# Numerators of an attention stage: two matmuls of 64 channels by 128 tokens per unit in place of four of 64 by 64

## The chip, the cores and the metric

The kernel runs on one core of one Trainium2 chip. The metric is the device time of one execution in microseconds (us). A core has a TensorE (in the profile PE for its matmuls, PEld for its weight loads), a VectorE (DVE), a ScalarE (ACT), a GpSimd (POOL) and a queue engine (SP) that here only issues transfers. A matmul multiplies a stationary operand ("weights", loaded by a LDWEIGHTS instruction of its own) by a moving operand that is streamed past it, and writes to PSUM, which has eight banks.

## What is computed

Linear attention over 8 batches of 8 heads, 576 tokens and 64 channels, and then a feed-forward layer with a tanh GELU over all 4608 tokens:

```python
q_p, k_p = (phi(q), phi(k))                      # phi(x) = x + 1 if x > 0 else exp(x)
kv  = np.einsum('bhsd,bhse->bhde', k_p, v)
z   = np.sum(k_p, axis=2)
num = np.einsum('bhsd,bhde->bhse', q_p, kv)
den = np.einsum('bhsd,bhd->bhs', q_p, z)[..., None] + 1e-06
attn_out = num / den
...
h = x @ w_in                                     # 4608x512 by 512x2048
g = gelu_tanh(h)
out = g @ w_out                                  # 2048x512
```

The kernel adds a column of ones to v, so that one product gives the numerator (64 columns) and the denominator (column 65) of a head. This product, of phi(q) with the 64 by 65 matrix `kv` of its head, is called n below; the sum over tokens that makes that matrix is called kv.

## The kernel before

Each batch gives its first 512 tokens to an iteration of its own (j = 0 to 7); the remaining 64 tokens of the eight batches make a ninth one (j = 8). An iteration is 16 groups of h (four 128x128 by 128x512 matmuls each, line 384) and 16 groups of o (four such matmuls each, line 725): for j from 2 on, all of h and then o by blocks of 128 tokens. The attention of a later batch is put between these groups by hand: `at(j, slot, fn)` keeps a function for a slot, and `run` calls it when the loop of `iteration` gets there. Nothing is scheduled by a planner: every engine runs its instructions in the order in which the program issues them, and semaphores hold it only for data and for free buffers.

`plan_attention(b)` puts the attention of batch b, for b = 3 to 7, at slot 17 of iteration b - 1, which is behind the second group of o. For b = 8 it puts the attention of the ninth iteration (the remaining tokens) at slot 17 of iteration 7. Each time it calls `nab_quads(qt_cs, bs, kv_b)`, which issues, one behind the other on TensorE,

- n: 16 units (c, i, a), one for each block c of 128 tokens and each pair of heads 2a + i, with four matmuls each: t for two halves of 64 tokens, s for the two heads of the pair. The weights are 64 channels by 64 tokens of the transposed phi(q) (`qt`, line 324), the moving operand is the 64 by 65 matrix of the head (`kv_of_head`, line 325), and the output goes to 64 partitions of a bank, s = 0 and s = 1 to different banks. Six units fill a pair of banks, and the last four go to a pair of their own (`n_pair`).
- kv of the batch after, where there is one (b = 3 to 6): 72 matmuls with weights of 64 tokens by 64 channels and a moving operand of 64 by 65 (`kv_paired`, line 249), four at a time on the four quarters of the array.

The function that `nab_quads` returns, `x_of`, then divides the numerators by their denominators on VectorE (lines 282 and 283), issues the four transposing transfers of the result on SP (line 665) and copies kv out of PSUM (line 347).

The halves t exist because in the ninth iteration a block of 128 tokens holds 64 tokens of one batch and 64 of the next, and so `bs[c]` names two batches and the two halves need different matrices. For b = 3 to 7 `bs[c]` is (b, b).

Of the kernel before, what the change touches and what calls it, by code (L numbers as in the profile page):

```python
# [15 lines left out]
def kernel(  # L16
# [20 lines left out]
    P = 128  # L37
    HP = P // 2
# [40 lines left out]
    def bank(name, shape, dt=FP32):  # L79
        return ps_b.tile(shape, dt, name=name, tag="b")  # L80

    def pair_of_banks(name):
        return ps_a.tile([P, 2, 512], FP32, name=name, tag="a")
# [159 lines left out]
    def kv_paired(b, ii, kv_of):  # L243
        kp, vp = phi["k", b], vp_paired(b)
        for j in range(J):
            for s in range(2):
                for a in range(2):
                    r, u = slice(HP * a, HP * (a + 1)), 2 * ii + s
                    nc.tensor.matmul(  # L249
                        kv_of(a, ii)[HP * s : HP * (s + 1)],  # L250
                        lhsT=kp[r, j, u, :],
                        rhs=vp[r, j, u, :],
                        start=(j == 0),
                        stop=(j == J - 1),
                        skip_group_check=True,
                    )
# [15 lines left out]
    def kv_of_head(b, s, i):  # L272

        r = slice(HP * s, HP * (s + 1))
        return kvs[b][r, i, :] if b > 2 else kvbds[b][r, i, E * s : E * (s + 1)]

    def divide(x_v, n_v):

        heads = tuple(slice(None) for _ in n_v.shape[:-1])
        shape = list(n_v.shape[:-1])  # L280
        r = psm.tile(shape, FP32, name="r" + "".join(str(d) for d in shape[1:]))
        nc.vector.reciprocal(r, n_v[heads + (D,)])  # L282
        nc.vector.tensor_tensor(  # L283
            x_v,
            n_v[heads + (slice(0, D),)],
            r[heads + (None,)].to_broadcast(shape + [D]),
            op=ALU.mult,
        )
# [20 lines left out]
    def nab_quads(qt_cs, bs, kv_b):  # L309

        ns = [[bank("n_ps", [P, 6 * E]) for _ in range(2)] for _ in range(2)]
        n_pair = pair_of_banks("n_ps")
        ns.append([n_pair[:, s] for s in range(2)])
        units = [(c, i, a) for c in range(C) for i in range(2) for a in range(2)]
        for n, (c, i, a) in enumerate(units):
            g = n // 6
            for t in range(2):
                for s in range(2):  # L320
                    cs = slice(HP * t, HP * (t + 1))
                    nc.tensor.matmul(  # L322
                        ns[g][s][cs, E * (n - 6 * g) : E * (n - 6 * g + 1)],
                        lhsT=qt_cs[c][HP * s : HP * (s + 1), 2 * a + i, cs],
                        rhs=kv_of_head(bs[c][t], s, 2 * a + i),
                        skip_group_check=True,
                    )
        if kv_b is not None:
            for ii in range(2):
                kv_paired(kv_b, ii, lambda a, ii: n_pair[:, a, E * (4 + ii) : E * (5 + ii)])  # L330

        def x_of(transposed):
            x = pxs.tile([P, C, d_model], BF16, name="xs")
            x_v = x.rearrange("p c (i s a d) -> p s (c i) a d", s=2, a=2, d=D)
            for g in range(2):
                for s in range(2):
                    divide(
                        x_v[:, s, 3 * g : 3 * (g + 1)],
                        ns[g][s].rearrange("p (k a e) -> p k a e", a=2, e=E),
                    )  # L340
                for c in ((0,), (1, 2))[g]:
                    transposed(c, x[:, c])
            n_v = n_pair[:, :, 0 : 4 * E].rearrange("p s (k a e) -> p s k a e", a=2, e=E)
            divide(x_v[:, :, 6:8], n_v)
            transposed(3, x[:, 3])
            if kv_b is not None:
                nc.vector.tensor_copy(
                    out=kvs[kv_b].rearrange("p (a i) e -> p a i e", a=2),
                    in_=n_pair[:, :, 4 * E : 6 * E].rearrange("p a (i e) -> p a i e", e=E),
                )  # L350

        return x_of
# [314 lines left out]
    def plan_attention(b):  # L667


        def attention():  # L670
            if b < B:
                bs = [(b, b)] * C
                x_of = nab_quads([qts[b][:, c] for c in range(C)], bs, b + 1 if b + 1 < B else None)
                x_of(lambda c, x: transposed_x(b, c, x))
            else:
                x_of = nab_quads(rest_qt, [(2 * m, 2 * m + 1) for m in range(C)], None)
                x_of(
                    lambda m, x: nc.sync.dma_start_transpose(
                        out=xt_rest[:, :, P * m : P * (m + 1)], in_=x
                    )  # L680
                )

        at(b - 1, 17, attention)
# [145 lines left out]
```

## Time and profile before

| | before |
|---|---|
| median of 4 runs | 283.92 us (283.90 to 284.55) |
| the profiled execution: its own time | 284.09 us |
| the profiled execution: its span | 282.3 us |
| mean granted TensorE clock | 0.998 |
| TensorE matmuls at line 322 (n) | 384, in six stretches |
| of these, batches 3 to 7 | 320, in five stretches |
| TensorE weight loads at line 322 | 384 |
| TensorE matmuls at line 249 (kv), behind an n | 288, in four stretches |

The span goes from the first to the last instruction of the program; the time of an execution has 1.8 us more around it. In the views, a line of a timeline gives the start and the length of a group of like instructions in us, the engine, the source line, the operation, output<-inputs, the shapes and the count; in brackets stands idle time before it. The length of a group runs to the end of its last instruction, and a matmul's end is modelled: successive matmuls overlap. "64*64" and "128*128" are the part of the array that an instruction uses, rows by columns. Some records of matmuls can be missing from a trace.

### The profile page before, as it was taken

The numbers are of one execution on the slowest core, as the hardware profiler recorded it, in microseconds if no ns is written. First come the engines' busy times: TensorE is split into PE (matmuls) and PEld (weight loads), VectorE is DVE, ScalarE is ACT, GpSimd is POOL, SyncE is SP. The second block draws the span as 40 slices with busy tenths as digits, with TensorE's granted clock in tenths as the row PEclk, the third lists the DMA queues.
The fourth block names the chain that finished last, engine by engine and source line by source line (L and its number), as shares of the span: only waits on it lengthen the run. The fifth ranks groups of instructions, "written<-read, shape, count | busy, mean of one in ns | idle before, by whom it ended". The sixth has DMA issues, their size and how long they took to land.

```text
span 282.3 us, 5435 instructions
## 1 busy us (share of the span) xinstructions
PE 273.6 (97%) x2311; PEld 135.4 (48%) x2341; DVE 102.6 (36%) x177; ACT 164.1 (58%) x224; POOL 15.0 (5%) x21
## 2 busy tenths in 40 slices
PE   8799999999999999999999999999999999999995
PEld 3474455445444544454445444544444444444444
DVE  3850386334955850356034640350114001400001
ACT  4678878785986915692569346832682364026400
POOL 3147200000000000000000000000000000000000
PEclk9999999999999999999999999999999999999999
DMA  7999999967999987907695640066405300420022
GB/s 244 401 406 396 411 401 404 404 250 219 176 386 266 297 152 216 377 22 170 179 386 122 155 129 0 2 118 179 115 2 148 114 0 2 138 85 0 2 74 74
DMA packets 59591, 53.83 MB, mean 191 GB/s; under 512 B 35760, under 2 KB 45360, under 8 KB 59568
## 3 DMA queue, kind: packets, MB, share of 16 engines
q1 hardware_dynamic: 56784, 44.58, 52.1%
q10 hardware_dynamic: 2784, 8.91, 8.8%
q8 instruction: 18, 0.29, 0.4%
q14 instruction: 5, 0.04, 0.0%
HBM read 36.70 MB, written 9.44 MB: 163 GB/s over the span
## 4 chain that ended last, share of the span: by engine, by line
PE 93%; DMA 3%; issue 1%; SPq 1%; DVE 1%; ACT 0%
PE h_ps L384 44%; PE o_ps L725 44%; DMA v_x<-in_v_dram 3%; PE n_ps L322 1%; PE kv_ps L249 1%; PE n_ps L249 1%; PE n_ps L265 1%; PE t_ps L377 1%; SPq L95 1%; SPq L100 0%; PE t_ps L530 0%; DVE vp L238 0%; DVE x L367 0%; DVE kvbd L261 0%; DVE o_sb L686 0%
## 5 line engine op out<-in xcount | busy, mean ns | idle before, releaser
L725 PE MATMUL o_ps<-w_out_sb,g 128*128 128x512 bf16 (+2 forms) x588 | 126.0, 367 | 1.6 <-issue 0.9
L384 PE MATMUL h_ps<-xt,w_in_sb 128*128 128x512 bf16 (+1 forms) x556 | 113.2, 359 | 0.5 <-issue 0.2
L394 ACT ACTIVATE g<-h_ps 128x512 bf16<-128x512 f32 x144 | 84.4, 600 | 36.5 <-PE h_ps L384 35.0
L384 PEld LDWEIGHTS <-w_in_sb 128*128 128x128 bf16 x628 | 58.5, 98 | 64.7
L725 PEld LDWEIGHTS <-g 128*128 128x128 bf16 x608 | 57.4, 98 | 63.4
L686 ACT COPY o_sb<-o_ps 128x512 f32<-128x512 f32 (+1 forms) x19 | 10.8, 575 | 65.7 <-PE o_ps L725 52.6
L686 DVE COPY o_sb<-o_ps 128x512 f32<-128x512 f32 (+1 forms) x19 | 12.2, 645 | 50.5 <-PE o_ps L725 45.6
L282 DVE RECIPROCAL r<-n_ps 128x6 f32<-128x6 f32 (+2 forms) x43 | 8.2, 191 | 59.8 <-PE n_ps L322 54.3
L227 DVE TENSOR_SCALAR k_p<-k_x 128x2304 bf16<-128x2304 f32 (+1 forms) x9 | 11.0, 1221 | 24.9 <-DMA k_x<-in_k_dram 24.9
L283 DVE TENSOR_TENSOR xs<-n_ps,r 128x384 bf16<-128x384 f32 (+1 forms) x30 | 17.5, 584 | 1.0
L219 ACT ACTIVATE k_e<-k_x 128x2304 bf16<-128x2304 f32 (+1 forms) x9 | 17.1, 1902 | 1.0 <-DMA k_x<-in_k_dram 0.9
L219 ACT ACTIVATE q_e<-q_x 128x2048 bf16<-128x2048 f32 (+1 forms) x9 | 15.5, 1719 | 3.0 <-DMA q_x<-in_q_dram 2.9
L227 DVE TENSOR_SCALAR q_p<-q_x 128x2048 bf16<-128x2048 f32 (+1 forms) x9 | 9.9, 1102 | 13.4 <-DMA q_x<-in_q_dram 13.4
L384 PE MATMUL h_ps<-xt_rest,w_in_sb 128*128 128x512 bf16 x63 | 13.9, 379 | 0.1
L233 DVE TENSOR_TENSOR q_p<-q_p,q_e 128x2048 bf16<-128x2048 bf16 (+1 forms) x9 | 9.9, 1100 | 6.9 <-ACT q_e L219 6.8
L407 ACT ACT_TABLE_LOAD x9 | 11.5, 1283 | 0.2
L233 DVE TENSOR_TENSOR k_p<-k_p,k_e 128x2304 bf16<-128x2304 bf16 (+1 forms) x9 | 11.0, 1220 | 1.2 <-ACT k_e L219 0.8
L238 DVE CAST vp<-v_x 128x2304 bf16<-128x2304 f32 (+1 forms) x9 | 11.0, 1223 | 0.6 <-DMA v_x<-in_v_dram 0.6
L219 ACT ACT_TABLE_LOAD x8 | 10.3, 1283 | 0.1
L416 PE MATMUL w_ps<-warm 128*128 128x512 bf16 x31 | 9.0, 450 | 1.2 <-DVE warm L181 1.2
L139 POOL CAST w_in_sb<-w_st 128x512 bf16<-128x512 f32 (+2 forms) x6 | 7.6, 1269 | 14.7 <-DMA w_st<-in_moe_w_in_dram 14.7
L283 DVE TENSOR_TENSOR x<-n_ps,r 128x512 bf16<-128x512 f32 (+1 forms) x13 | 7.9, 609 | 0.4
(50 smaller groups left out, 77.5 us busy)
## 6 DMA issues: line engine op xcount, KB each, us to landing
out_dram<-o_sb ACTq DMA_DIRECT2D x16, 512.0 KB, 3.2
k_x<-in_k_dram SPq DMA_DIRECT2D x7, 1152.0 KB, 7.2
v_x<-in_v_dram SPq DMA_DIRECT2D x7, 1152.0 KB, 11.8
q_x<-in_q_dram SPq DMA_DIRECT2D x6, 1024.0 KB, 9.5
w_st<-in_moe_w_in_dram SPq DMA_DIRECT2D x3, 1024.0 KB, 13.3
q_x<-in_q_dram SPq DMA_DIRECT2D x4, 512.0 KB, 8.8
w_st<-in_moe_w_out_dram SPq DMA_DIRECT2D x2, 1024.0 KB, 12.7
w_st<-in_moe_w_out_dram SPq DMA_DIRECT2D x4, 512.0 KB, 11.2
```

What stands on the lines that cost most here:

```text
L219: nc.scalar.activation(o, i, AF.Exp)
L227: nc.vector.tensor_scalar(o, i, 1.0, 1.0, op0=ALU.add, op1=ALU.max)
L233: nc.vector.tensor_tensor(p, p, e, op=ALU.min)
L238: fn(out=vp_paired(b)[:, :, us, 0:D].rearrange("p j u d -> p u j d"), in_=ld["v", b][:, us].rearrange("p u (j d) -> p u j d", d=D),)
L282: nc.vector.reciprocal(r, n_v[heads + (D,)])
L283: nc.vector.tensor_tensor(x_v, n_v[heads + (slice(0, D),)], r[heads + (None,)].to_broadcast(shape + [D]), op=ALU.mult,)
L384: nc.tensor.matmul(h_ps[:, ts], lhsT=w_in_sb[:, c, P * m : P * (m + 1)], rhs=xt[:, c, ts], start=(c == 0), stop=(c == KM - 1), skip_group_ ...
L394: nc.scalar.activation(g[:, m, :], h_ps, AF.Gelu_apprx_tanh)
L407: nc.scalar.preload_act_table_set("gelu_apprx_tanh_and_others")
L416: nc.tensor.matmul(w_ps, lhsT=warm[:, 0:P], rhs=warm)
L686: (nc.scalar.copy if on_scalar else nc.vector.tensor_copy)(dst, src)
L725: nc.tensor.matmul(o_ps, lhsT=g[:, m, P * t : P * (t + 1)], rhs=w_out_sb[:, m, fs], start=(m == 0), stop=(m == MM - 1),)
```

## The change

Where both halves of a block belong to the same batch (batches 3 to 7), the loop over t is run once, with all 128 tokens as weights: a unit is two matmuls (s = 0, 1) of 64 channels by 128 tokens with an output of 128 partitions, in place of four of 64 by 64 with an output of 64 partitions. The ninth iteration's n stays as it was, and so does kv.

```diff
         for n, (c, i, a) in enumerate(units):
             g = n // 6
-            for t in range(2):
+            one = bs[c][0] == bs[c][1]
+            for t in range(1 if one else 2):
                 for s in range(2):
-                    cs = slice(HP * t, HP * (t + 1))
+                    cs = slice(0, P) if one else slice(HP * t, HP * (t + 1))
                     nc.tensor.matmul(
                         ns[g][s][cs, E * (n - 6 * g) : E * (n - 6 * g + 1)],
                         lhsT=qt_cs[c][HP * s : HP * (s + 1), 2 * a + i, cs],
                         rhs=kv_of_head(bs[c][t], s, 2 * a + i),
```

`HP` is 64, `P` 128 and `E` 65. The five stretches have 160 matmuls and 160 weight loads fewer in all.

## The prediction

> **What bounds the kernel now.** I read the page first, its busy times and its chain of waits, which is followed back from the last instruction:
>
> ```profile
> PE 273.6 (97%) x2311; PEld 135.4 (48%) x2341; DVE 102.6 (36%) x177; ACT 164.1 (58%) x224; POOL 15.0 (5%) x21
> PE 93%; DMA 3%; issue 1%; SPq 1%; DVE 1%; ACT 0%
> ```
>
> TensorE is busy for 97% of the span and is 93% of the chain. A busy PE alone would not prove that it is the bound, so I looked at the same chain in order of time, around one place of the change:
>
> ```profile
> 93.29 0.15 issue
> 93.44 0.76 PE n_ps L322 x64
> 94.20 0.68 PE n_ps L249 x72
> 94.88 0.16 issue
> 95.04 10.74 PE o_ps L725 x49
> ```
>
> From here to the end the chain never leaves TensorE: n, kv, o, h follow each other with no wait for another engine. A nanosecond saved or lost in n is one of the whole time, unless it makes somebody late (see below). Third came the timeline of TensorE around all five places. Three of them, and a kv alone (behind an o and ahead of an o, with no n) for comparison:
>
> ```profile
> 39.87 0.78 PE L249 MATMUL kv_ps<-vp,k_p 64*64 64x65 bf16 x72
> 40.58 0.39 PE L725 MATMUL o_ps<-w_out_sb,g 128*128 128x512 bf16 x1
> ```
> ```profile
> 121.80 0.81 PE L725 MATMUL o_ps<-w_out_sb,g 128*128 128x512 bf16 x3
> 122.54 0.76 PE L322 MATMUL n_ps<-kv,qt 64*64 64x65 bf16 x64
> 123.12 0.86 PE L249 MATMUL n_ps<-vp,k_p 64*64 64x65 bf16 x72
> ```
> ```profile
> 180.75 0.76 PE L322 MATMUL n_ps<-kv,qt 64*64 64x65 bf16 x64
> 181.33 0.84 PE L249 MATMUL n_ps<-vp,k_p 64*64 64x65 bf16 x72
> ```
> ```profile
> 209.83 0.76 PE L322 MATMUL n_ps<-kv,qt 64*64 64x65 bf16 x64
> 210.75 1.46 PE L725 MATMUL o_ps<-w_out_sb,g 128*128 128x512 bf16 x6 [0.16 <-issue]
> ```
>
> The reader is to see three things. First, the same 72 kv matmuls take 0.78 us alone and 0.86 (batch 6: 0.84) behind n. Second, n to its last start: each of these lengths has a tail of 0.19 (a 64x65 matmul's own duration), so n takes 0.57 from first to last start, and kv follows at 122.54 + 0.58. Third, the price of a change between the array as a whole and its four quarters. The last of three 512-wide matmuls starts at 121.80 + 0.81 - 0.38 = 122.23 and n at 122.54, 0.31 later, where 512-wide matmuls follow each other in (0.81 - 0.38)/2 = 0.215: 0.09 lost. Back again, at the kv alone, the last kv starts at 39.87 + 0.78 - 0.19 = 40.46 and o at 40.58: 0.12, of which some 0.03 is that last matmul's own streaming, so 0.09 again. The 0.16 of "issue" behind the other stretches is no further cost: the weights of two o matmuls are loaded 0.12 behind the last kv there, and the record of the first of these matmuls is missing (line 725 has 608 weight loads and 588 matmuls).
>
> **Pace within n.** The single records of batch 3's n show their starts: after a first gap of 0.05, the units of four follow each other in about 32 ns for thirteen units (93.49 to 93.87), then there is a break of some 55 ns, and the last units and all of kv come in single instructions, one load and one matmul each 8 to 9 ns, with more such breaks. I read this as two regimes: while instructions stand ready in TensorE's queue, the array sets the pace; when the queue has run dry, the delivery of instructions does, at about 9.3 ns for a load and its matmul (kv behind n: 0.86 - 0.19 = 0.67 for 72). kv alone, with a full queue, takes 0.59 for its 72.
>
> **The change, part by part.** (1) n, five stretches: 32 loads and 32 matmuls instead of 64 and 64. Each unit still streams 65 columns through both row halves. No row of this trace has 64 rows by 128 columns, so its pace is bounded. From below: 65 columns at the rate of a 512-wide matmul, 65/512 x 0.215 = 27 ns. From above: two full 128-column loads with their matmuls one after the other, by the nearest row
>
> ```profile
> L725 PE MATMUL o_ps<-w_out_sb,g 128*128 128x128 bf16 x32 | 1.9, 219 | 0.0
> L725 PEld LDWEIGHTS <-g 128*128 128x128 bf16 x608 | 57.4, 98 | 63.4
> L322 PEld LDWEIGHTS <-qt 64*64 64x64 bf16 x320 | 3.3, 106 | 2.1 <-issue 2.1
> ```
>
> 1.9/32 = 59 ns each, so 119 for two. I take 32, the pace of the present units: the same 65 columns in the same row halves, half the instructions. That asks for a load of 128 columns to hide under 32 ns of streaming. For it speaks that a load of 128 columns is recorded at 98 ns and one of 64 at 106, so twice the weights are not loaded more slowly when the array is whole. n then takes 0.05 + 14 x 0.032 = 0.50 from first to last start, and delivery (32 pairs at 9.3 ns, 0.30) keeps ahead: the break of 55 ns goes, and the queue is still full behind n. (2) A new change of shape, from 64 by 128 to 64 by 64, between n and kv in batches 3 to 6; batch 7 has no kv. Bounds: 0 (both split the rows alike) to 0.09. I take 0.09, so 0.125 from the last n to the first kv, since the two changes that the trace has cost 0.09 each, in either direction. (3) kv behind it, with the queue full: 0.78, as alone, instead of 0.86 (0.84). Bounds: 0.78 to 0.86.
>
> Batches 3 to 5: 0.50 + 0.125 + 0.78 = 1.405 against 122.54 to 123.98, 1.44: -0.035 each. Batch 6: 1.405 against 1.42: -0.015. Batch 7: 0.50 + 0.19 = 0.69 against 0.76: -0.07. Sum: -0.19 us. On the profiled execution (284.09, of which 282.3 is span) that gives 283.90; it lay 0.17 over the median of 283.92, so for the median 283.73, say 283.7.
>
> (4) Nothing else moves. The divisions start with a finished pair of banks, a little earlier or later, on a VectorE that is at it until 97.9; the last of batch 3's four transposing transfers is issued at 99.6 and lands at the latest 5.7 later (the longest of the four), at 105.3, while the h that reads them starts at 107.07: 1.8 us of cover, and a later n shifts that h, on the same engine, by the same amount. Banks, their order and the semaphores stay as they are.
>
> The Trainium skill speaks against the change in two places. "TensorEngine Tiling (Array Packing)", Key Properties, says that changing the tiling mode drains the TensorE; the 0.09 rows above agree for whole against quarters, and by this page part (2) costs as I took it. "TensorE: Matmul & The Clock Gate", section LDWEIGHTS, puts a load at its columns over 1.2 GHz, which would be 107 ns for 128 columns and an estimated +5 us for the five stretches; but by that rule 64 columns would need 53 ns, and this trace has four such loads in every 32. Its section on weight-path modes has a fast load for full 128-column weights of 16-bit types, which fits 98 against 106 ns; no run here shows it on half the rows.
>
> **Rivals.** *A: the load of 128 columns on half the rows sets the pace* (slower). For it: today's loads bring 64 columns per quarter in 32 ns, and nothing shows how much of these 32 is load; if all of it, 128 columns need 64, and the whole array's row gives 59. Two row halves that take turns would come to the same. Against: the 98 ns above. The five stretches have 70 gaps, so each ns per unit is 0.07 us. The gain of 0.19 is gone at 35 ns per unit, and from 43 ns on the kernel is slower by over 0.57. At 59: 27 x 0.07 = 1.89, less 0.19: +1.7, so 285.6. At 50: +1.07, 285.0.
>
> *B: no drain between n and kv*, since both split the rows in two: 4 x 0.09 less, -0.55 in all: 283.4; with the lower bound of 27 ns per unit as well (-0.35), 283.0. For it: the row split is the same. Against: both recorded changes cost 0.09.
>
> *C: kv gets no faster*, because its pace of 9.3 ns is its own and the full queue does not last: 4 x 0.05 (n and drain 0.625 against 0.58) - 0.07 = +0.13: 284.05. For it: kv needs 144 instructions, more than are likely to stand ready. Against: the kv alone shows 0.78 with the same 144.
>
> That the change does nothing is no rival: the pairs in `bs` are equal for batches 3 to 7, so all five stretches change.
>
> **How the numbers follow.** Forecast 0.45, A 0.33, B 0.10, C 0.12. 0.2% is 0.57 us, about what a measurement of this kernel can tell from no change. The forecast's own range, 29 to 35 ns per unit, is 283.5 to 283.95; it and C lie within 0.2%, as do the mild ends of A and B. Faster by more needs most of B's gains together, or an unforeseen one: 0.15. Slower: nearly all of A, 0.32. Same: 0.53. The range of 8 in 10 goes from 283.1, which takes in most of B, to 285.5, which leaves out A's dearer half.
>
> **What would show it.** Line 322 should have 160 matmuls of 64*128 and a stretch's length (with its tail) near 0.69; a length over 0.9 is A, and its load's mean duration then should stand well above 106 ns. From the last n to the first kv 0.12 is the drain, 0.03 is B. kv of 0.78 shows the full queue, 0.86 is C. Batch 7's stretch has neither kv nor a new change of shape and shows n alone. I would be wrong outright if TensorE waited for another engine behind n.

## The result, and the profile after

| | before | after |
|---|---|---|
| median | 283.91 us (60 runs, 283.79 to 284.55) | 283.59 us (42 runs, 283.48 to 283.97) |
| ratio | | 0.9988, 95% interval 0.9984 to 0.9993 |
| the profiled execution: its time, its span | 284.09, 282.3 | 283.56, 281.8 |

The change makes the kernel 0.32 us faster between the medians, 0.11%; 283.7 had been forecast, in a range from 283.1 to 285.5. The gain is smaller than the 0.2% up to which the prediction speaks of the same time, but the interval of the ratio excludes no change. Of all the runs in this document two fell far out, 486.81 and 1028.11 us, both of the changed kernel with the divisions in another order, whose ratio below leaves them out.

The page after, its busy times and its chain:

```profile
PE 273.5 (97%) x2151; PEld 135.0 (48%) x2181; DVE 102.7 (36%) x177; ACT 164.4 (58%) x224; POOL 15.0 (5%) x21
PE 93%; DMA 3%; issue 1%; SPq 1%; DVE 1%; ACT 0%
```

160 matmuls and 160 weight loads fewer, and TensorE is the bound as before. The timeline of TensorE after, around the attention of batches 4 and 7 (the same columns as before the change: start, length, engine, line, what; n is now line 323 and o line 726):

```profile
122.28 0.66 PE L323 MATMUL n_ps<-kv,qt 64*128 64x65 bf16 x32
122.88 0.78 PE L249 MATMUL n_ps<-vp,k_p 64*64 64x65 bf16 x72
```
```profile
209.40 0.66 PE L323 MATMUL n_ps<-kv,qt 64*128 64x65 bf16 x32
210.22 2.10 PE L726 MATMUL o_ps<-w_out_sb,g 128*128 128x512 bf16 x9 [0.16 <-issue]
```

n's length goes from 0.76 to 0.66 and kv's behind it from 0.86 to 0.78, and between the last n (122.28 + 0.66 - 0.19 = 122.75) and the first kv (122.88) there is now a gap of 0.12, where 0.01 was. From first to last start, by the single records, in us:

| | n before | n after | last n to first kv, before | after | kv before | kv after | all, after less before |
|---|---|---|---|---|---|---|---|
| batches 3, 4, 5 | 0.568 | 0.475 | 0.011 | 0.119 | 0.669 | 0.586 | -0.068 each |
| batch 6 | 0.569 | 0.475 | 0.010 | 0.119 | 0.644 | 0.586 | -0.043 |
| batch 7 | 0.567 | 0.474 | | | | | -0.093 |

The sum is -0.34 us, beside -0.32 between the medians; the interval of the ratio is -0.20 to -0.45. The two profiled executions differ by 0.53, but 0.19 of this is there before any changed instruction (the kv of batch 1 starts at 39.87 before and at 39.68 after), so that part is the start of this one execution and not the change. What is left is 0.34 again.

### The profile page after: what moved, and what is told of

It reads as the page before. It is cut to its first block, busy times and chain, and to the rows that moved or that the text cites. A ratio compares the mean times of both kernels' runs of the same rounds, so it can differ in the third digit from the quotient of the medians.

```text
span 281.8 us, 5115 instructions
## 1 busy us (share of the span) xinstructions
PE 273.5 (97%) x2151; PEld 135.0 (48%) x2181; DVE 102.7 (36%) x177; ACT 164.4 (58%) x224; POOL 15.0 (5%) x21
## 4 chain that ended last, share of the span: by engine, by line
PE 93%; DMA 3%; issue 1%; SPq 1%; DVE 1%; ACT 0%
PE h_ps L385 44%; PE o_ps L726 44%; DMA v_x<-in_v_dram 3%; PE n_ps L323 1%; PE n_ps L249 1%; PE kv_ps L249 1%; PE n_ps L265 1%; PE t_ps L378 1%; SPq L95 1%; SPq L100 0%; PE t_ps L531 0%; DVE vp L238 0%; DVE x L368 0%; DVE kvbd L261 0%; DVE o_sb L687 0%
```

## The experiments

Two questions were left. What sets the pace within n, the load or the streaming? And why does kv behind n take less time now? The theory at first was the prediction's: streaming sets the pace, and kv used to find an empty instruction queue. Times of other kernels stand against runs of the kernel before on the same chip (284.15 in the first four, 284.09 in the rest).

**The loads by themselves.** Ahead of n, the same loads again, each with a matmul of 16 columns in place of 65; the second kernel does this with the old 64-column loads.

```diff
+        if bs[0][0] == bs[0][1]:
+            for n, (c, i, a) in enumerate(units):
...
+                        nc.tensor.matmul(
+                            ns[g][s][cs, E * (n - 6 * g) : E * (n - 6 * g) + 16],
+                            lhsT=qt_cs[c][HP * s : HP * (s + 1), 2 * a + i, cs],
+                            rhs=kv_of_head(bs[c][t], s, 2 * a + i)[:, 0:16],
```

> The changed kernel with a pass ahead of n in each of the five stretches: the same 32 loads of 64 channels by 128 tokens, but each followed by a matmul of only 16 of the 65 columns (n then writes over its output; nothing is left out). In the changed kernel a unit of n, two loads and two matmuls, takes 29 ns. Theory (the streaming of 65 columns sets that pace and the load hides under it): with 16 columns the pace falls well below 29 ns, to about the load's own length or the delivery of four instructions at 4.7 ns each, 10 to 20 ns per unit; the pass takes 0.2 to 0.3 us from first to last start. Rival (the load of 128 columns sets the 29 ns): the pass keeps the pace of n, 0.45 us or more.

> The kernel before with a pass ahead of n in the same five stretches: the same 64 loads of 64 channels by 64 tokens, each with a matmul of 16 columns (nothing is left out). A unit is four loads and four matmuls; n's own unit took 32 ns. If the load of 64 columns in the plain form sets the 32 ns, the first units of this pass, whose instructions stand ready, keep about 30 ns; if the streaming sets it, they fall to 20 ns or less. Later units are held by delivery, eight instructions at 4.7 ns, 37 ns, in both cases. n behind it starts with an empty queue: 0.60 to 0.68 us from first to last start in place of 0.57.

The timeline of TensorE with 128-column loads, and that with 64-column loads (batch 4 both):

```profile
122.85 0.56 PE L323 MATMUL n_ps<-kv,qt 64*128 64x16 bf16 x32
123.27 0.65 PE L335 MATMUL n_ps<-kv,qt 64*128 64x65 bf16 x32
```
```profile
126.57 0.68 PE L323 MATMUL n_ps<-kv,qt 64*64 64x16 bf16 x64
127.10 0.75 PE L334 MATMUL n_ps<-kv,qt 64*64 64x65 bf16 x64
```

From start to start the pass takes 0.414 with 128-column loads and 0.527 with 64-column ones, 0.039 and 0.052 of it the first gap: 0.375/15 = 25.0 ns and 0.475/15 = 31.7 ns per unit, and the single records have these gaps one like the other. Neither expectation was met as a whole. In the new shape the pass needs 25 ns for a unit, more than the 10 to 20 of the theory, but less than the 31 that a unit of n takes there (records: three units of 29, then one of 35, again and again). In the old shape the pass keeps the whole pace of n, 32, with a quarter of the columns; and n behind it took 0.553 us from first to last start, not the 0.60 to 0.68 that were expected of an empty queue.

So within n the kernel before was not bound by its streaming, but by its weight loads, or by a cost that a load and its matmul have whatever the columns: every load here has a matmul behind it, and no run tells the two apart. Below, "the loads" stands for both. Two loads of 128 columns on half the rows go faster than four of 64 columns on a quarter, 25.0 against 31.7 ns. The instruction records of the traces show a difference between them: a load of 64 by 128 reads its columns as four pieces of 32, as every load of 128 columns on the whole array does, and a load of 64 by 64 reads one piece of 64. The changed n, at 31, is slower than its pass; what adds the 6 ns was not tried (the prediction's lower bound, by streaming, was 27). Behind the pass it keeps its pace.

Each of the two kernels was run once. The pass cost 1.6 us in the first (285.75), where five times 0.41 less the change's own 0.34 makes 1.7. It cost 8.4 in the second (292.52), far over five times 0.53; the last section comes back to this.

**Row halves in turn.** All of n's matmuls of s = 0 first, then all of s = 1:

```diff
-        for n, (c, i, a) in enumerate(units):
+        one = bs[0][0] == bs[0][1]
+        for n, (c, i, a), s in (
+            [(n, u, s) for s in range(2) for n, u in enumerate(units)]
+            if one
+            else [(n, u, s) for n, u in enumerate(units) for s in range(2)]
+        ):
...
```

> The changed kernel with the order of n turned: all 16 matmuls of the heads s = 0 (channels on partitions 0 to 63), then all 16 of s = 1 (partitions 64 to 127). Nothing is left out. Theory: the two matmuls of a unit run at the same time because they lie on different row halves; with neighbours on the same half they follow each other at 29 ns each, n takes 32 x 0.029 = 0.93 us instead of 0.47, and the kernel is 5 x 0.46 = 2.3 us slower than the changed one, about 285.9. That is the price that was put on row halves taking turns. Rival (TensorE works both halves whatever the order, or the pace comes from instructions): n stays near 0.47 and the time near 283.6.

The timeline of TensorE, batch 4:

```profile
123.02 1.05 PE L326 MATMUL n_ps<-kv,qt 64*128 64x65 bf16 x32
124.00 0.78 PE L249 MATMUL n_ps<-vp,k_p 64*64 64x65 bf16 x72
```

n takes 1.05 - 0.19 = 0.86, 28 ns for each of its 32 matmuls, somewhat less than the 0.93 expected. The time is 285.75 (ratio 1.0056, 1.0043 to 1.0070): 1.6 over the kernel before, and so 1.9 over the changed one, which is 5 x 0.385. The two matmuls of a unit run at the same time because they lie on different halves of the rows and stand next to each other; the order of the loop is part of the gain.

**Batch 7 alone.**

```diff
-            one = bs[c][0] == bs[c][1]
+            one = bs[c][0] == bs[c][1] == B - 1
```

> The change for batch 7 alone, whose n has no kv behind it; batches 3 to 6 as before. Theory: n shrinks by 0.09 us there with no new change of shape to pay, and everything else stands: -0.09 against before, 0.25 over the changed kernel. Rival (the gain comes from the whole of the program, for instance from fewer instructions fetched or from the start): -0.2 or more, or nothing.

283.99 against 284.15, ratio 0.9995 (0.9986 to 1.0004): too little to be told from no change by the times. In the trace n of batch 7 goes to 0.477 and the four other stretches stay at 1.248 and 1.222, so the gain is local, as expected.

**kv ahead of n.** In both kernels the block that issues kv is moved ahead of the loop of n.

```diff
+        if kv_b is not None:
+            for ii in range(2):
+                kv_paired(kv_b, ii, lambda a, ii: n_pair[:, a, E * (4 + ii) : E * (5 + ii)])
         for n, (c, i, a) in enumerate(units):
```

> The kernel before with kv issued ahead of n instead of behind it (nothing is left out). Theory (kv behind n is slow because n has emptied the instruction queue): the lack moves to n. kv takes 0.585 us from first to last start, as alone, n 0.64 to 0.68 instead of 0.57, the stretch stays at 1.25 and the time at 283.9. Rival (kv behind n is slow for a reason of its own, such as VectorE reading the banks of n at the same time): kv 0.585 and n 0.57, the stretch 1.16, four times 0.08 less, 283.6.

> The changed kernel with kv issued ahead of n (nothing is left out). Theory: n's four instructions per 29 ns are delivered in 19, so n takes 0.47 even behind an emptied queue, kv 0.585, and the change of shape from 64 by 64 to 64 by 128 costs the same 0.09 as the other way round: the stretch stays at 1.18, the time at 283.6. Rival (n needs the full queue too): n 0.55 or more, and 0.3 us slower. Rival (only one direction drains): the stretch 1.09, 0.36 us faster.

The timeline of TensorE of the kernel before with kv first, batch 4:

```profile
122.61 0.78 PE L249 MATMUL n_ps<-vp,k_p 64*64 64x65 bf16 x72
123.20 0.77 PE L325 MATMUL n_ps<-kv,qt 64*64 64x65 bf16 x64
```

Here the theory failed. n behind kv takes 0.77 - 0.19 = 0.58, hardly more than with a full queue, the stretch is 1.168 in place of 1.248, and the time 283.80, ratio 0.9988 (0.9979 to 0.9997): the ratio of the change itself, by moving three lines. An empty queue alone was not what cost kv its 0.08. The timeline of the changed kernel with kv first, batch 4:

```profile
122.23 0.78 PE L249 MATMUL n_ps<-vp,k_p 64*64 64x65 bf16 x72
122.94 0.67 PE L326 MATMUL n_ps<-kv,qt 64*128 64x65 bf16 x32
```

Here the order makes no difference (283.76, ratio 0.9988, 0.9979 to 0.9997): by the records kv takes 0.586, the gap is 0.125, and n takes 0.475. The change of shape costs about the same in this direction.

**What the breaks are.** A signal is here the raising of the semaphore for which VectorE's divisions wait. Counted from 0, the records of the kernel before have the same two breaks in every stretch of n and kv: at matmuls 54 and 55 of n, and at 14 and 15 of kv behind it, two gaps of some 16 and 34 ns follow each other where 8 to 9 is usual, and five matmuls later comes one of 25. The matmuls that signal VectorE are 22 and 23 (the last two of the first six units, one for each bank) and 46 and 47, so a break follows a pair of signals by 32 matmuls: 23 + 32 = 55, 47 + 32 = 79, which is 15 of kv. With kv first, n's first pair is number 95 of the stretch and its break is at 127; the second pair's would be at 151, when the stretch is over. This made a new theory, that a signal holds up the delivery of instructions, and a rival to it, that VectorE's reading of PSUM does.

First with one signal less per group, by dividing s = 1 first:

```diff
-                for s in range(2):
+                for s in (1, 0):
                     divide(
```

> The kernel before with VectorE dividing the bank of s = 1 ahead of that of s = 0, so that the last matmul of a group of six units signals once for both banks instead of the last two signalling once each (nothing is left out). In the traces so far the breaks in n and kv come exactly 32 matmuls behind such a pair of signals (matmuls 22 and 23, break at 54 and 55; 46 and 47, break at 15 of kv), whatever stands there. Theory (each signal holds up the delivery of instructions by some 26 ns, felt 32 matmuls later where the queue has run dry): half the break goes, 0.03 us, twice per stretch with kv and once in batches 7 and 8: about -0.25 in all, 283.8 against 284.1. Rival (VectorE's reading of PSUM holds up TensorE): as before, since it reads the same at the same time.

Its timeline of TensorE, batch 4:

```profile
122.40 0.74 PE L322 MATMUL n_ps<-kv,qt 64*64 64x65 bf16 x64
122.95 0.84 PE L249 MATMUL n_ps<-vp,k_p 64*64 64x65 bf16 x72
```

n goes from 0.568 to 0.542 and kv from 0.669 to 0.643, 26 ns for each signal taken away, and the time to 283.81, ratio 0.9990 (0.9981 to 0.9998): -0.28 where -0.25 was expected.

The kernel before holds a comparison of the same kind, without any edit. The last matmul of n, number 63, signals too in batches 3 to 5, but not in batch 6. Behind it, at matmuls 31 and 36 of kv, batches 3 to 5 have gaps of 17 and 25 ns; batch 6 has neither, and its kv is 0.025 us shorter (0.644 against 0.669). Three signals, 46, 47 and 63, at 26 ns each make the 0.08 us that kv behind n takes longer than kv alone.

Then with the last pair of banks divided first, in three kernels (the one before, that with batch 7 alone changed, and the changed one):

```diff
+            divide(x_v[:, :, 6:8], n_v)
+            transposed(3, x[:, 3])
             for g in range(2):
...
-            divide(x_v[:, :, 6:8], n_v)
-            transposed(3, x[:, 3])
```

> The kernel before with VectorE dividing the last pair of banks first and the two groups of six units behind it, so that no matmul inside n signals any more (nothing is left out; the divisions start about 1 us later, behind kv). Theory of the signals: no breaks; n and kv together 1.13 to 1.16 us from first to last start instead of 1.25, n of batches 7 and 8 0.51 to 0.53 instead of 0.57: -0.4 to -0.55 in all, 283.6. If the divisions are too late for the next h, TensorE waits there and the time is above 284. Rival (the breaks belong to the fetching of instructions, not to signals): the breaks stay at the same matmuls.

> As the run before, and batch 7 alone with 64 channels by 128 tokens: batches 3 to 6 then have no signals inside n and no change of shape between n and kv, and batch 7 has n in 0.47. Theory: 1.13 to 1.16 us per stretch against 1.18 in the changed kernel, and 0.02 to 0.05 less than the run before: the fastest of all, 0.1 to 0.3 below the changed kernel's gain, about 283.5 against 284.1 before.

> The changed kernel with the same order of the divisions (no signals inside n). Theory: in the changed kernel n uses up its instructions at half the pace, the queue stays filled and the hold-ups by signals are hidden already: the five stretches stay at 1.18 and 0.47, only n of batch 8 gains its 0.05; 283.7 against 284.1 before. Rival (the drain or the pace of n contains the signals): the stretches get shorter by 0.05 or more.

The premise failed: the trace shows the same signals at 22, 23, 46 and 47, though nobody needs them sooner than the last one. But the divisions did move, and so these runs tell the rival apart. The kernel before in this order, TensorE and then VectorE, batch 4:

```profile
122.53 0.76 PE L322 MATMUL n_ps<-kv,qt 64*64 64x65 bf16 x64
123.11 0.86 PE L249 MATMUL n_ps<-vp,k_p 64*64 64x65 bf16 x72
```
```profile
124.04 0.21 DVE L282 RECIPROCAL r<-n_ps 128x8 f32<-128x8 f32 x1 [6.34 <-PE n_ps L249]
```

VectorE is idle for 6.34 us up to 124.04 and touches no bank until kv's last modelled end (123.97) is past, and yet n and kv have their 0.76 and 0.86, with the breaks at the same matmuls. So it is not VectorE's reading. The breaks stand 32 matmuls behind n's signals in either order of n and kv, halve with one signal of a pair, and are missing where a signal is missing. Times: 284.16 (ratio 1.0004, 0.9995 to 1.0012), 283.96 (0.9998, 0.9990 to 1.0007) and 283.82 (0.9989, 0.9980 to 0.9998), each as its kernel without the new order, and no sign of the later divisions in TensorE's waits.

In the changed kernel the signals are still there (matmuls 10, 11, 22, 23), but no break follows them. The likely reason is that n needs its four instructions in 31 ns there instead of its eight in 32, so that a hold-up of two times 26 ns is made up before the queue has nothing to give; no run tried this by itself.

**kv on its own, six groups of o later**, in both kernels:

```diff
-                x_of = nab_quads([qts[b][:, c] for c in range(C)], bs, b + 1 if b + 1 < B else None)
+                x_of = nab_quads([qts[b][:, c] for c in range(C)], bs, None)
...
         at(b - 1, 17, attention)
+        if b + 1 < B:
+            at(b - 1, 23, kv_in_pair, b + 1)
```

> The kernel before with kv taken away from behind n and put six groups of o later, so that the queue is full again (nothing is left out; kv goes to banks of its own after n's are free). Theory: kv takes 0.585 us from first to last start instead of 0.67, and a change of shape into and one out of the quarters comes on top, 0.19 in four places: 0.10 each or +0.4 us in all, 284.3. Rival (kv is slow for its own reason or n for its own): kv 0.67 again and +0.75 us, 284.65. Rival (a change of shape costs nothing of its own, the gaps are an empty queue): 0.4 us faster.

> The changed kernel with kv six groups of o later (nothing is left out). Theory: kv had a full queue already, 0.585 as before the split; the change of shape between n and kv (0.12 from start to start) is replaced by one out and one in (0.125 + 0.09): +0.10 in four places, +0.4 over the changed kernel, 284.0. Rival (a drain between 64 by 128 and 64 by 64 is dearer or cheaper than the other ones): by that much less or more.

The timeline of TensorE of the first, batch 4:

```profile
122.67 0.76 PE L322 MATMUL n_ps<-kv,qt 64*64 64x65 bf16 x64
123.37 5.35 PE L727 MATMUL o_ps<-w_out_sb,g 128*128 128x512 bf16 x24
128.65 0.78 PE L249 MATMUL kv_ps<-vp,k_p 64*64 64x65 bf16 x72
129.36 1.04 PE L727 MATMUL o_ps<-w_out_sb,g 128*128 128x512 bf16 x4
```

kv is back at 0.78 and n keeps its own break, so the 0.08 isn't kv's own. (The time alone, 284.66, would not tell this: against 284.09 it lies between the theory's +0.4 and the rival's +0.75.) The last n starts at 123.24 and o at 123.37, 0.13; the last o starts at 128.34 and kv at 128.65, 0.31 for what takes 0.216 within o. From batch 4 to batch 5 this kernel needs 29.24 us where the one before needs 29.10: +0.14 each, somewhat over the 0.10 that I had put down, and 284.66 in all (ratio 1.0021, 1.0012 to 1.0030). The changed kernel pays 0.11 each, 284.21 (1.0003, 0.9994 to 1.0012), 0.46 over its own -0.34. The changes of shape cost about the same wherever they stand.

## Why the prediction was right, and where it was not

- **The bound** was read rightly: what n and kv saved came through to the end, -0.34 us over the five stretches beside -0.32 between the medians.
- **(1) n's pace** is the term that was mis-sized: 0.50 forecast, 0.475 measured. Five times 0.025 is 0.13 of the 0.15 by which the sum (-0.19 against -0.34) fell short. I took the present 32 ns per unit for the new shape too, as the streaming of the same 65 columns. But these 32 were not the streaming: the pass with 16 columns keeps them, at 31.7. The new shape's pass needs 25, and a unit of the new n 31. That 31 came out so near to 32 is luck, since the two have different limits. The first gap went from 0.052 to 0.038. The rest of n's gain is the break, which I did expect to go (the prediction read it as 55 ns in one piece; by the records it is two gaps of some 50 ns together and one of 25 five matmuls later, and costs 26 ns per signal). The estimate of +5 us, from a load of 107 ns, did not come: the pass has two loads of 128 columns in 25.0 ns.
- **(2) The change of shape** between n and kv: 0.125 forecast, 0.119 measured, and 0.125 where kv comes first. Rival B (no drain) is out. Here "TensorEngine Tiling (Array Packing)", Key Properties, in the Trainium skill agrees with the trace for half against quarter arrays too, where the gaps are 0.119 and 0.125.
- **(3) kv** of 0.78, right, and rival C out. The reason that I gave is only half of it, so the number owes something to luck. A queue that has run dry does deliver a load and its matmul in some 8 ns (the 9.3 had the breaks in it), but that is no slower than kv alone, 0.585/71 = 8.2; the 0.08 came from the breaks, and these follow n's signals. "TensorE: Matmul & The Clock Gate", in its section on the per-tile semaphore tail, fits each signal at 26.3 ns; the two runs here show 26 ns per signal, felt 32 matmuls later.
- **(4) Nothing else moved**: the divisions could even start 1 us later, in the runs with the other order, at no cost.
- **Rival A** (the load sets the pace) had 0.33. Its premise fits the kernel before, where the pass of the loads takes all of the 32 ns; its conclusion, that twice the columns take twice as long, was wrong. The row that spoke against it, 98 ns for a load of 128 columns and 106 for one of 64, was the right one to trust: the new loads read their columns in the same four pieces as those of 98. After the change that line reads

```profile
L323 PEld LDWEIGHTS <-qt 64*128 64x128 bf16 x160 | 2.7, 94 | 2.1 <-issue 2.1
```

## What to carry to other kernels

Before small matmuls are repacked, ask what sets their present pace: a pass of the same loads with few columns tells the streaming from the rest, and here it turned the weighing of the main rival round. Where a stretch of tiny matmuls runs at the pace of its instructions, look at which of them signal and what stands behind (here it was 32 matmuls behind): moving kv ahead of n, three lines, gave as much (-0.29) as the new shape did (-0.32), and the two do not add up. Matmuls on different halves of the rows that are to run at once should stand next to each other; here the same matmuls in another order took 0.86 in place of 0.47.

## What was not expected of the hardware

TensorE can stand still for microseconds with no semaphore, as far as the profile shows, to wait for. The second kernel with a pass ahead of n, in the timeline of TensorE, at batch 3 and at batch 5:

```profile
93.50 0.68 PE L323 MATMUL n_ps<-kv,qt 64*64 64x16 bf16 x64
94.02 0.75 PE L334 MATMUL n_ps<-kv,qt 64*64 64x65 bf16 x64
94.59 0.65 PE L249 MATMUL n_ps<-vp,k_p 64*64 64x65 bf16 x47
98.50 0.41 PE L249 MATMUL n_ps<-vp,k_p 64*64 64x65 bf16 x25 [3.26 <-issue]
```
```profile
157.28 0.48 PE L249 MATMUL n_ps<-vp,k_p 64*64 64x65 bf16 x29
159.61 0.54 PE L249 MATMUL n_ps<-vp,k_p 64*64 64x65 bf16 x43 [1.85 <-issue]
```

TensorE stops in the middle of kv for 3.3 us, after 2 x (64 + 64 + 47) = 350 instructions in 1.6 us, and for 1.9 us at batch 5, after 314; the view gives no semaphore for it ("issue"). Five passes of 0.53 and what the stops add to kv from first to last start (3.46 and 2.01) make 8.1 of the 8.4 us. The queue that brings instructions moved one packet of 16 KB between 94 and 99 us, at 96.2 to 97.1, and one at batch 5, at 157.3 to 158.2; both times TensorE went on 1.4 us after the packet's end. That the stops were for these packets is an inference from the times, and no run here tried it. The number of instructions does not decide by itself: batches 4 and 6 of the same kernel ran all 400 of theirs without a stop. The stretch without the pass (272 instructions) never stopped, at any batch.
